# First four weight loads issued from ScalarE's queue instead of SyncE's, in a strided-attention and gated feed-forward kernel

## The chip, the cores and the metric

The kernel runs on one core of one Trainium2 chip. The metric is device time in microseconds (us) of one execution; the time of a kernel is the median over its runs. A smaller number is better.

## The reference, cut to what matters

Eight batches of eight heads attend over 576 positions with head size 64. Four heads use a local causal mask of 32 positions, four a strided causal mask. The heads are concatenated to a token matrix of 4608 x 512, which goes through two matrix products with a gate between them.

```python
scores = (1.0 / np.sqrt(D)) * np.matmul(q, k.transpose(0, 1, 3, 2))
mask_local = (rel >= 0) & (rel < 32)
mask_strided = (rel >= 0) & (pos[None, :] % 32 == pos[:, None] % 32)
attn = softmax(np.where(mask_of_head, scores, -1e9))
x = np.matmul(attn, v)            # rearranged to 4608 x 512
h = x @ w_in                      # 512 x 2048
g = h * np.clip(h + 3.0, 0.0, 6.0) / 6.0
out = g @ w_out                   # 2048 x 512
```

The two weight matrices come as 64-bit floats, q, k and v as 32-bit floats.

## The kernel before, in words

**Order of the work.** The kernel records every operation with the engines that may run it, a cost, a due time and the keys that it reads and writes (`op`, line 74). `Plan.emit` (line 91) then walks a list scheduler over the records, with the costs and due times as they are written, and so fixes the order of the instructions on each engine. The chip runs each engine's list strictly in that order; what an instruction really waits for is decided by semaphores. A change of one record's engine or cost can therefore move instructions on every engine, far from the record itself. Where the planner sees a gap on TensorE early on, it puts in a filler matmul on the identity (line 1580).

**Attention.** A pair is two heads of one batch. The pairs of batch 0 are worked in the order 0, 2, 1, 3 (`TURNS`); pairs 0 and 1 are local, 2 and 3 strided. For these four, q and k are loaded plainly and turned upright by TensorE (line 372), copied out of PSUM by ScalarE or VectorE (lines 514, 516), multiplied to scores (lines 605, 613), and the softmax goes back and forth: VectorE masks and takes the maximum (638, 652), GpSimd subtracts it (656), ScalarE takes the exponential (660), VectorE sums and inverts (666, 669), GpSimd normalises (673). For strided pairs ScalarE copies the scores out in four pieces for each head (631), and GpSimd adds the mask (648). The weights of the softmax are turned by TensorE and ScalarE for pairs 0 and 1 (372, 730) and by VectorE for pairs 2 and 3 (692). The product with v (389, 745) is written out as a high part by ScalarE (427) and a low part by VectorE (430); these are the tiles x.

**v of the first four pairs.** `load_v` (line 558) issues it from SyncE: six transfers for a local pair (lines 378 and 381), four for a strided one (line 567). These loads are recorded with the key "gate", which a small memset on VectorE (line 644) writes, so the planner puts none of them ahead of it.

**Weights.** `weight_part` (line 261) is called 32 times, for 16 blocks of w_in and 16 of w_out, in the order of `k`. One block is 128 x 512 in 64-bit floats. `load` (line 268) issues its transfer; the first sixteen blocks also wait for "gate" in the plan. The first four blocks (k below 4) are those of w_in for the first quarter of the hidden units; they have due times of their own. Then each block is turned into 32-bit floats by two ScalarE operations (282, 286) and one of VectorE (290, the join), and split into a high part (ScalarE 304 or GpSimd 306) and a low part (GpSimd 309).

**Feed-forward.** `ffn` (line 828) works batch 0 first: a chunk `fc` of 128 hidden units is the sum of four groups of three matmuls, one group for each pair's x (866, 867, 868, tile ph); the first four chunks are begun together. The gate is a ScalarE and a VectorE operation (786, 789); the result is split into a high part on ScalarE (800) and a low part on GpSimd (804, tile gl), and the second product goes to the tiles acc (843, 844, 845, of which 845 needs gl). Later batches are worked in the same manner or, for batches 3 to 7, by a recursive scheme with fewer products.

**Queues.** In the program before, SyncE issues all transfers but the k of the first two pairs, which ScalarE issues at the start. The transfers of both queues take turns on eight completion semaphores, so that each transfer waits for the one eight places earlier in the program.

## Time and profile before

| what | value |
|---|---|
| median of 3 runs | 872.61 us (871.39 to 873.68) |
| the profiled execution | 868.6 us, its span 866.8 us |
| mean granted TensorE clock in it | 0.997 |
| busy, of the span | TensorE 97%, GpSimd 71%, ScalarE 64%, VectorE 62% |
| bytes moved | 179.12 MB, mean 207 GB/s |

The profile shows one execution. PE is TensorE, DVE VectorE, ACT ScalarE, POOL GpSimd, and SPq and ACTq are the queues that issue transfers. In a row of the timeline stand the start, the duration, the engine, the line, the operation, the tile written and the tile read, the shape and the count; square brackets hold the idle time ahead of it and what ended that. Names such as L274 are lines of the kernel before; in the changed program all lines behind the new constant are one higher.

### The profile page before, as it was taken

What the parts mean: (1) busy time and instruction counts of PE and PEld (TensorE: products, weight loads), DVE (VectorE), ACT (ScalarE), POOL (GpSimd) and SP (SyncE); (2) the same over time, 40 slices, a digit from 0 to 9 for tenths busy, and PEclk for the clock granted to TensorE, in tenths of its full rate; (3) what the DMA queues carried; (4) which work ended last, traced back from release to release, by engine and by line L of the source; (5) the groups of instructions that cost most, each with busy time, mean ns of one, the idle gap of its engine ahead of it and who ended that gap; (6) DMA issues with size and microseconds to landing.
All of it is one profiled execution on the core that took longest, in us unless ns stands there. A gap on an engine that the chain in (4) does not pass through costs nothing.

```text
span 866.8 us, 18953 instructions
## 1 busy us (share of the span) xinstructions
PE 844.6 (97%) x6956; PEld 680.0 (78%) x6956; DVE 539.1 (62%) x899; ACT 558.8 (64%) x1240; POOL 615.8 (71%) x612
## 2 busy tenths in 40 slices
PE   9899999999999999999999999999999999999996
PEld 7667777878888887888888878788888778888884
DVE  6878877534444437554545663566767988555586
ACT  4777665877877965887768755777644645454441
POOL 5798785678448878676577995565974987767573
PEclk9999999999999999999999999999999999999998
DMA  6999714889874346889999998787666667866636
GB/s 156 314 210 271 195 32 119 250 246 286 251 201 115 104 118 170 230 222 249 264 251 266 341 287 226 212 240 195 183 200 184 193 179 222 242 197 194 182 122 146
DMA packets 323308, 179.12 MB, mean 207 GB/s; under 512 B 182864, under 2 KB 300368, under 8 KB 323216
## 3 DMA queue, kind: packets, MB, share of 16 engines
q1 hardware_dynamic: 318564, 176.27, 72.4%
q10 hardware_dynamic: 4652, 1.64, 0.9%
q8 instruction: 55, 0.90, 0.4%
q14 instruction: 37, 0.30, 0.1%
HBM read 136.97 MB, written 40.89 MB: 205 GB/s over the span
## 4 chain that ended last, share of the span: by engine, by line
PE 79%; POOL 7%; DVE 5%; ACT 3%; DMA 3%; issue 2%; SPq 0%; POOLq 0%; DVEq 0%; ACTq 0%
PE P L1139 9%; PE P L1141 8%; PE P L1140 8%; PE cP L1462 5%; PE cP L1463 5%; PE cP L1464 5%; PE acc L843 4%; PE acc L845 4%; PE acc L844 4%; PE ph L866 4%; PE ph L868 3%; PE ph L867 3%; PE acc L1224 3%; PE acc L1225 3%; PE acc L1226 3%; PE pv L400 2%
## 5 line engine op out<-in xcount | busy, mean ns | idle before, releaser
L1480 DVE SCALAR_TENSOR_TENSOR C<-cP,C 128x512 f32<-128x512 f32 x96 | 65.7, 687 | 40.3 <-PE cP L1464 39.5
L804 POOL TENSOR_TENSOR gl<-u,gh 128x512 fp32r<-128x512 f32 x48 | 64.6, 1351 | 23.9 <-ACT gh L800 13.2
L1151 DVE TENSOR_TENSOR G<-P,G 128x512 f32<-128x512 f32 x64 | 44.0, 689 | 57.9 <-PE P L1141 49.5
L845 PE MATMUL acc<-wo,gl 128*128 128x512 f32 x192 | 75.5, 393 | 2.5 <-POOL gl L804 2.2
L1139 PE MATMUL P<-B_T,wr 128*128 128x512 f32 x192 | 75.4, 393 | 2.3 <-DVE G L1151 1.6
L843 PE MATMUL acc<-wo,gh 128*128 128x512 f32 x192 | 76.9, 400 | 0.7 <-POOL wo L309 0.7
L844 PE MATMUL acc<-wo,gh 128*128 128x512 f32 x192 | 75.0, 391 | 0.2 <-POOL wo L309 0.2
L1141 PE MATMUL P<-B_T,wr 128*128 128x512 f32 x192 | 74.8, 389 | 0.0
L1140 PE MATMUL P<-B_T,wr 128*128 128x512 f32 x192 | 74.7, 389 | 0.0
L1377 POOL TENSOR_TENSOR sp<-G,sp 128x512 fp32r<-128x512 f32 x34 | 47.5, 1410 | 25.7 <-ACT sp L1373 25.7
L1146 ACT COPY G<-P 128x512 f32<-128x512 f32 x64 | 37.6, 587 | 43.4 <-PE P L1141 43.0
L673 POOL TENSOR_TENSOR e<-e,st 128x144 f32<-128x144 f32 (+1 forms) x64 | 43.6, 683 | 29.3 <-DVE st L669 21.2
L789 DVE SCALAR_TENSOR_TENSOR u<-u,ph 128x512 f32<-128x512 f32 x48 | 32.6, 681 | 42.0 <-ACT u L786 41.9
L866 PE MATMUL ph<-x,wi 128*128 128x512 f32 x128 | 52.3, 409 | 3.5 <-DVE u L789 1.9
L708 ACT COPY atloc<-e 32x192 f32<-32x192 f32 x144 | 50.8, 353 | 3.8 <-DVE e L698 1.4
L868 PE MATMUL ph<-x,wi 128*128 128x512 f32 x128 | 50.4, 394 | 1.1 <-POOL wi L309 1.1
L867 PE MATMUL ph<-x,wi 128*128 128x512 f32 x128 | 50.1, 391 | 0.4 <-DVE x L430 0.4
L666 DVE TENSOR_REDUCE st<-e 128x8 f32<-128x152 f32 (+1 forms) x64 | 26.9, 426 | 35.2 <-ACT e L660 18.9
L1139 PE MATMUL P<-B_B,wr 128*128 128x512 f32 x120 | 48.2, 401 | 0.1
L1140 PE MATMUL P<-B_B,wr 128*128 128x512 f32 x120 | 46.9, 390 | 0.0
L1141 PE MATMUL P<-B_B,wr 128*128 128x512 f32 x120 | 46.8, 390 | 0.0
L845 PEld LDWEIGHTS acc<-wo,gl 128*128 128x128 f32 x192 | 36.0, 188 | 12.2 <-POOL gl L804 4.6
(605 smaller groups left out, 2650.0 us busy)
## 6 DMA issues: line engine op xcount, KB each, us to landing
wr<-dA SPq DMA_DIRECT2D x72, 256.0 KB
or<-do SPq DMA_DIRECT2D x32, 512.0 KB
wr<-dSu SPq DMA_DIRECT2D x48, 256.0 KB
wr<-dSv SPq DMA_DIRECT2D x48, 256.0 KB
or<-do SPq DMA_DIRECT2D x48, 256.0 KB
rawi<-in_moe_w_in_dram SPq DMA_DIRECT2D x16, 512.0 KB
rawo<-in_moe_w_out_dram SPq DMA_DIRECT2D x16, 512.0 KB
do<-wo SPq DMA_DIRECT2D x16, 512.0 KB
```

The source lines that it names most:

```text
L708: nc.scalar.copy(at[PAD * (a + h):PAD * (a + h) + PAD, :, rows], e[rows, :, PAD * h:PAD * h + PAD])
L804: (nc.vector if tail else nc.gpsimd).tensor_tensor(out=to, in0=src(), in1=tiles[gk[0]].bitcast(F32), op=ALU.subtract)
L843: nc.tensor.matmul(acc, gh, woh, start=fc == 0, stop=False)
L844: nc.tensor.matmul(acc, gh, wol, start=False, stop=False)
L845: nc.tensor.matmul(acc, gl, woh, start=False, stop=end)
L866: nc.tensor.matmul(ph, wih, xh, start=n_ == 0, stop=False)
L867: nc.tensor.matmul(ph, wih, xl, start=False, stop=False)
L868: nc.tensor.matmul(ph, wil, xh, start=False, stop=n_ == NCC - 1)
L1139: nc.tensor.matmul(ph, wh, xh, start=fresh and k == 0, stop=False, skip_group_check=not fresh)
L1140: nc.tensor.matmul(ph, wh, xl, start=False, stop=False, skip_group_check=not fresh)
L1141: nc.tensor.matmul(ph, wl, xh, start=False, stop=k == 1, skip_group_check=not fresh)
L1480: nc.vector.scalar_tensor_tensor(out=tiles[ck], in0=tiles[bank], scalar=1.0 / 6.0, in1=tiles[ck], op0=ALU.mult, op1=ALU.add)
```

## The change

The loads of the first four weight blocks are recorded for ScalarE instead of SyncE, at a cost of 0.45 instead of 0.53 in the plan, and are issued from ScalarE's queue. Due times, reads, writes and all other records stay.

```diff
 AHEAD = 27.0
+ONACT = 4
 OPEN = 6.0
...
-            nc.sync.dma_start(raw, src.bitcast(I32).rearrange("p (n t) -> p n t", t=2))
+            (nc.scalar if k < ONACT else nc.sync).dma_start(raw, src.bitcast(I32).rearrange("p (n t) -> p n t", t=2))
...
-        op("SP", 0.53, load, reads=["gate"] if k < 16 else [], writes=[key], due=(-49, -48.99, -48.8, -48.79)[k] if k < 4 else ...)
+        op("ACT" if k < ONACT else "SP", 0.45 if k < ONACT else 0.53, load, reads=["gate"] if k < 16 else [], writes=[key], due=(-49, -48.99, -48.8, -48.79)[k] if k < 4 else ...)
```

What moves is seen in the programs. First ScalarE, at the start of pair 0's softmax, before; qt and kt are the upright q and k of pair 1, e0 and e1 the two heads' scores, ps0_20 and ps1_21 the raw scores of pair 2:

```order
L514 COPY qt0_1_255<-qp0_11_380 128x3x96
L514 COPY kt0_1_256<-kp0_10_403 128x3x96
L660 ACTIVATE e0_130<-e0_130 96x6x64
L631 COPY e0_130<-ps0_20_425 32x8x18 x4
L660 ACTIVATE e1_228<-e1_228 96x6x64
L631 COPY e1_228<-ps1_21_426 32x8x18 x4
```

And the same place of the changed program; rawi00 to rawi03 are the four weight blocks:

```order
L515 COPY qt0_1_255<-qp0_11_380 128x3x96
L275 DMA rawi00_423<-in_moe_w_in_dram 128x1024
L275 DMA rawi01_427<-in_moe_w_in_dram 128x1024
L275 DMA rawi02_464<-in_moe_w_in_dram 128x1024
L275 DMA rawi03_468<-in_moe_w_in_dram 128x1024
L661 ACTIVATE e0_130<-e0_130 96x6x64
L661 ACTIVATE e1_228<-e1_228 96x6x64
L632 COPY e0_130<-ps0_20_429 32x8x18 x4
```

The four issues stand ahead of pair 0's two exponentials, which now follow each other; the copy of kt that stood there went to VectorE.

On SyncE the v of the four pairs now stands in one row. This is the changed program from the second head of pair 0 on, with the semaphores that each transfer waits for; 0 to 7 behind DMAHW are the eight completion semaphores, and the weight blocks 00 to 03 hold numbers 0, 2, 4 and 6:

```order
L379 DMA v0_01_239<-in_v_dram 32x64 [waits DMAHW7_49]
L382 DMA v0_01_239<-in_v_dram 64x8x64 [waits DMAHW0_49]
L382 DMA v0_01_239<-in_v_dram 64x9x64 [waits DMAHW1_49]
L568 DMA v0_2_241<-in_v_dram 18x2x512 [waits DMAHW2_49]
L568 DMA v0_2_241<-in_v_dram 18x2x512 [waits DMAHW3_49]
L568 DMA v0_2_241<-in_v_dram 18x2x512 [waits DMAHW4_49]
L568 DMA v0_2_241<-in_v_dram 18x2x512 [waits DMAHW5_49]
L379 DMA v0_10_251<-in_v_dram 32x64 [waits DMAHW6_49]
```

Before, two weight loads stood between the v of pair 2 and that of pair 1, and two between pair 1 and pair 3. Now four of the v transfers wait until a weight block of the other queue has landed.

GpSimd, where the first low part of the gated result (gl0_0, for chunk 0) is made, before; wo is a block of w_out, wi10 and wi11 are blocks of the second quarter of w_in:

```order
L306 CAST wo02_985<-fo02_944 128x512
L309 TENSOR_TENSOR wo01_977<-fo01_915,wo01_977 128x512
L309 TENSOR_TENSOR wo02_985<-fo02_944,wo02_985 128x512
L309 TENSOR_TENSOR wo03_997<-fo03_983,wo03_997 128x512
L804 TENSOR_TENSOR gl0_0_1031<-u0_0_1009,gh0_0_1026 128x512
L804 TENSOR_TENSOR gl0_1_1036<-u0_1_1014,gh0_1_1029 128x512
L306 CAST wi10_1051<-fi10_999 128x512
L309 TENSOR_TENSOR wi10_1051<-fi10_999,wi10_1051 128x512
```

And in the changed program:

```order
L307 CAST wo03_996<-fo03_976 128x512
L310 TENSOR_TENSOR wo02_993<-fo02_951,wo02_993 128x512
L310 TENSOR_TENSOR wo03_996<-fo03_976,wo03_996 128x512
L307 CAST wi10_1009<-fi10_998 128x512
L310 TENSOR_TENSOR wi10_1009<-fi10_998,wi10_1009 128x512
L307 CAST wi11_1032<-fi11_1007 128x512
L310 TENSOR_TENSOR wi11_1032<-fi11_1007,wi11_1032 128x512
L805 TENSOR_TENSOR gl0_0_1054<-u0_0_1021,gh0_0_1045 128x512
L805 TENSOR_TENSOR gl0_1_1061<-u0_1_1029,gh0_1_1052 128x512
```

Two whole weight blocks now stand ahead of gl0_0. On TensorE one group each of chunks 4 and 5 now stands ahead of the first acc. On TensorE there are three filler matmuls more in all (15 instead of 12): three instead of one ahead of the transposes of pair 3's k, none instead of one between the two heads' turned softmax of pair 0, six instead of three ahead of pair 2's values, and two instead of three ahead of those of pair 1. On VectorE the copy of pair 3's k (line 516) now stands ahead of pair 2's first maximum (652) instead of behind it, and the first weight block's join (290) behind both of pair 1's sums (666) instead of ahead of the second. Small exchanges of neighbours go on through about the first 70% of each engine's list; behind that the order is the old one.

More of the change, by code (lines that the diff above doesn't have):

```diff
@@ L309, in lo @@
             nc.gpsimd.tensor_tensor(out=part(1), in0=whole(), in1=part(0).bitcast(F32), op=ALU.subtract)
-        op("SP", 0.53, load, reads=["gate"] if k < 16 else [], writes=[key], due=(-49, -48.99, -48.8, -48.79)[k] if k < 4 else -48.4 + 0.01 * k if k < 6 else -2 + 0.1 * k if k < 16 else due - 20.0, early=7.0 if k < 16 else due - 30.0, after=1.6 if k < 16 else 1.25)
+        op("ACT" if k < ONACT else "SP", 0.45 if k < ONACT else 0.53, load, reads=["gate"] if k < 16 else [], writes=[key], due=(-49, -48.99, -48.8, -48.79)[k] if k < 4 else -48.4 + 0.01 * k if k < 6 else -2 + 0.1 * k if k < 16 else due - 20.0, early=7.0 if k < 16 else due - 30.0, after=1.6 if k < 16 else 1.25)
         op("ACT", 0.68, high, reads=[key], writes=[fkey], due=due - 5, room=LATE + 1.0)
```

## The prediction

> **What bounds the kernel now.** I read the page first, for the bound of the whole, then the busy time by stage, then the timeline of the first 60 us, where the change lies. From the page, the share of TensorE and the chain that ended last:
>
> ```profile
> PE 844.6 (97%) x6956; PEld 680.0 (78%) x6956; DVE 539.1 (62%) x899; ACT 558.8 (64%) x1240; POOL 615.8 (71%) x612
> PE 79%; POOL 7%; DVE 5%; ACT 3%; DMA 3%; issue 2%; SPq 0%; POOLq 0%; DVEq 0%; ACTq 0%
> ```
>
> TensorE bounds the run. Only the parts of the chain outside it, all told a fifth, can be shortened, and most of them lie early. The busy time by stage, with columns from:to, length, the busy time of PE, PEld, DVE, ACT and POOL, the granted clock, the DMA share and GB/s:
>
> ```profile
> 15.00:23.00 8.00, 8.00 (x266) 6.46 (x259) 5.80 (x16) 4.77 (x16) 4.10 (x8) 1.00 0.66 165
> 23.00:30.00 7.00, 6.29 (x141) 4.54 (x136) 6.78 (x19) 4.71 (x11) 2.86 (x4) 1.00 0.93 229
> 30.00:50.00 20.00, 17.01 (x176) 11.81 (x175) 13.64 (x29) 15.35 (x37) 18.27 (x22) 1.00 1.03 367
> 51.00:54.00 3.00, 1.73 (x7) 0.88 (x6) 2.04 (x4) 3.00 (x6) 2.70 (x3) 1.00 0.62 94
> 60.00:100.00 40.00, 38.36 (x368) 29.50 (x369) 32.97 (x60) 25.80 (x48) 34.34 (x33) 1.00 0.86 223
> 140.00:840.00 700.00, 695.30 (x5149) 564.49 (x5148) 411.92 (x656) 464.60 (x1055) 496.50 (x476) 1.00 0.75 213
> ```
>
> The reader is to see three stages. From 23 to 30 us VectorE is the full engine (6.78 of 7). From 30 to 50 it is GpSimd (18.27 of 20), with the transfers at their limit (share 1.03, 367 GB/s). From 60 us on TensorE is idle for only 1.64 of 40 us, and for 4.7 of the 700 us from 140 to 840. TensorE's 8.00 of 8 at the start is not all work:
>
> ```profile
> L1580 PE MATMUL idle<-ident x24: 486/486/1009, 2.8 to 30.8; 128*128 128x384 f32 x24
> ```
>
> These are the fillers, up to 30.8 us. So the change can earn only what TensorE loses before about 60 us, and whatever it earns there must get past VectorE and then GpSimd.
>
> **SyncE's row.** The issues of v and of the first weights:
>
> ```profile
> 13.20 0.33 SPq L378 DMA_DIRECT2D v<-in_v_dram  x1
> 17.94 1.64 SPq L567 DMA_DIRECT2D v<-in_v_dram  x4
> 19.62 0.84 SPq L274 DMA_DIRECT2D rawi<-in_moe_w_in_dram  x2
> 20.50 1.67 SPq L378 DMA_DIRECT2D v<-in_v_dram  x1
> 25.66 2.34 SPq L274 DMA_DIRECT2D rawi<-in_moe_w_in_dram  x2
> 28.11 1.40 SPq L567 DMA_DIRECT2D v<-in_v_dram  x4
> 29.55 4.22 SPq L274 DMA_DIRECT2D rawo<-in_moe_w_out_dram  x4
> ...
> rawi<-in_moe_w_in_dram SPq DMA_DIRECT2D x16, 512.0 KB
> ```
>
> The two pairs of weight issues take 0.84 + 2.34 = 3.18 us. Without them the first w_out load goes from 29.55 to 26.4. Against this stand the new waits: four v transfers wait for a weight block to land, and the rest of SyncE's list, every later load, is queued behind them. Four blocks are 2.1 MB, 5.7 us at the 367 GB/s of the full stage. Issued from 13.6 on, the fourth lands at 19.3 at best, and v of pair 1, which waits for it, would come up at 19.6: nothing lost. At worst it shares with all that is moved from 15 to 23 now (165 GB/s, 1.3 MB): 3.4 MB, 9.3 us, 22.9, and 3.3 us are lost. So w_out starts between 26.4 and 29.7, and I take the middle, 28.0. GpSimd takes up the first w_out block only at 44.08 (below), 14.5 us after its issue, so that neither end is on the path. If that cover went, it would be worth 1.6 us.
>
> The Trainium skill, "DMA: Bandwidth & Descriptors", section "Issuing engines are not separate DMA queues", says that transfers started from several engines run on the same 16 DMA engines, and that a second issuing engine saves only the time of issuing. By that rule the whole change is worth at most those 3.18 us of SyncE. The row from 15 to 23 agrees only in part: with a DMA share of 0.66 there is also room into which weights can be moved.
>
> **ScalarE's row.** The place that takes the four issues, and the first use of a weight block:
>
> ```profile
> 12.36 1.19 ACT L514 COPY qt<-qp 128x288 f32<-128x288 f32 x2 [1.49 <-PE qp L372]
> 14.80 0.54 ACT L660 ACTIVATE e<-e 96x384 f32<-96x384 f32 x1
> 17.06 0.53 ACT L660 ACTIVATE e<-e 96x384 f32<-96x384 f32 x1
> ...
> 25.98 0.64 ACT L282 ACTIVATE fi<-rawi 128x512 f32<-128x512 f32 x1
> ```
>
> ScalarE is free at 13.55. At 0.42 us an issue (0.84 for two) it is done at 15.2, at 1.06 (4.22 for four, a full queue) at 17.8. I take 15.2, since the queue is empty. The first exponential starts at 15.2 instead of 14.80, the second at 15.8 instead of 17.06: pair 0 gains about a microsecond on GpSimd. At the other end the exponentials lose 3.0 and 1.3 us. The gain is not kept, since other engines' lists changed too.
>
> **Pair 2, on TensorE and VectorE.** One filler, three fillers, pair 2's first maximum, its second head's turning, and the first block's join:
>
> ```profile
> 16.94 0.91 PE L1580 MATMUL idle<-ident 128*128 128x384 f32 x2
> 23.71 2.20 PE L1580 MATMUL idle<-ident 128*128 128x384 f32 x6
> ...
> 18.09 0.29 DVE L652 TENSOR_REDUCE st<-e 128x8 f32<-128x144 f32 x1
> 25.09 1.75 DVE L692 STREAM_TRANSPOSE atstr<-e 32x256 f32<-32x256 f32 x4
> 28.57 1.26 DVE L290 SCALAR_TENSOR_TENSOR fi<-fi,rawi 128x512 int32<-128x512 int32 x1
> ```
>
> Three fillers (2.20) now run from 16.94, so pair 3's k is turned from 19.1. Its first half is there half a microsecond later, and VectorE's copy of it, about 0.5, ends near 20.2. Pair 2's first maximum, which now stands behind it, slips from 18.09 to 20.2, by 2.1. VectorE is full from then on, so the second head's turning ends at 28.9 instead of 26.84, and the join, now behind one more sum, starts at about 30.9 instead of 28.57, though the block has been in memory for some 10 us. At the least (the fillers hidden under the wait for VectorE's copies) the slip is 0.9.
>
> **GpSimd.** The low parts of the first block and of the block needed second, the block of w_out work, and the first two gl with what follows:
>
> ```profile
> 31.96 1.27 POOL L309 TENSOR_TENSOR wi<-fi,wi 128x512 fp32r<-128x512 f32 x1
> 39.41 1.29 POOL L309 TENSOR_TENSOR wi<-fi,wi 128x512 fp32r<-128x512 f32 x1
> 44.08 1.03 POOL L306 CAST wo<-fo 128x512 fp32r<-128x512 f32 x1 [0.80 <-issue]
> 46.79 0.64 POOL L306 CAST wo<-fo 128x512 fp32r<-128x512 f32 x1
> 47.39 4.30 POOL L309 TENSOR_TENSOR wo<-fo,wo 128x512 fp32r<-128x512 f32 x3
> 51.99 3.01 POOL L804 TENSOR_TENSOR gl<-u,gh 128x512 fp32r<-128x512 f32 x2 [0.30 <-ACT gh L800]
> 54.95 0.60 POOL L306 CAST wi<-fi 128x512 fp32r<-128x512 f32 x1
> 55.64 1.31 POOL L309 TENSOR_TENSOR wi<-fi,wi 128x512 fp32r<-128x512 f32 x1
> 61.52 0.82 POOL L656 TENSOR_TENSOR e<-e,st 128x144 f32<-128x144 f32 x2
> ```
>
> The first block starts late and the next ones are ready at once, so GpSimd closes its gaps: it has 1.7 idle us from 30 to 50 to close. I put the second-needed low part at 40.7 as before (39.41 + 1.29), between 39.0 and 42.2. Then come one more low part (1.29) and a normalising step (0.41): 42.4. The w_out work took from 44.08 to 51.69, 7.61 us; the new order has one more high part, 0.64, so it ends at 50.65. Two w_in blocks follow (0.60 + 1.31 each, 3.82) to 54.5, then the first gl (half of 3.01) to 56.0. TensorE at this place, and its pitch:
>
> ```profile
> 52.01 0.47 PE L843 MATMUL acc<-wo,gh 128*128 128x512 f32 x1 [0.65 <-POOL wo L309]
> 53.34 0.50 PE L845 MATMUL acc<-wo,gl 128*128 128x512 f32 x1 [0.62 <-POOL gl L804]
> 53.67 0.39 PE L843 MATMUL acc<-wo,gh 128*128 128x512 f32 x1
> 53.90 0.40 PE L844 MATMUL acc<-wo,gh 128*128 128x512 f32 x1
> ```
>
> The first matmul that needs gl moves from 53.34 to about 56.0, 2.6 later. By then TensorE has done two groups more (chunks 4 and 5), six matmuls of 0.23, 1.4 us. So it is 1.2 us behind. GpSimd, though, is ahead: it ends the second gl at 57.5 with 3.82 us of w_in done, which before would have ended at 55.0 + 3.8 = 58.8, so by 1.3. Of TensorE's 1.64 idle us from 60 to 100 I let this lead win back half, 0.8, between nothing and all.
>
> **The sum.** 1.2 - 0.8 = +0.4. The profiled execution took 868.6 us (span 866.8, 1.8 around it), 4.0 below the median of the runs shown. I forecast 869.0 for such an execution and 873.0 for the median. About 0.3%, 2.6 us, is what a measurement of this kernel can tell from no change: 870.0 to 875.2. The case's own range is +0.4 with -0.8 to +0.8 for the lead won back and -1.7 to +1.5 for GpSimd's place at 40.7, which hardly both end at their worst: 871.3 to 874.8.
>
> **The rivals.**
>
> Faster: the early weights reach TensorE. For it: the transfers have room (0.66), and the blocks' conversions, at 25.98 before, can start about 22.5. Against it: VectorE is full, and in its new order the join is late. If the slip is only 0.9 and GpSimd closes its 1.7, the first gl is ready at about 54.3: 1.0 late, against two groups of 1.4 done, and all of the 1.64 is won back: -2.0. If it is not late at all, -1.4 - 1.64 = -3.0, which is 869.6.
>
> Slower: GpSimd's detour ahead of the first gl. For it: the order puts 3.82 us there, and VectorE's joins now come in one row beside GpSimd, where such a step took 1.03 instead of 0.64 (44.08 and 46.79). If the seven w_out steps and four w_in steps each stretch by half of that 0.4, 2.2 is added to 1.2, and nothing is won back: +3.4, which is 876.0. It decides from the point where the first gl ends later than 53.3 + 1.4 + 2.6 = 57.3.
>
> No effect as meant: the v transfers wait for the weights' landing, and SyncE's list starts w_out at 29.7 as before. Since that is covered by 14 us, it gives the forecast's time.
>
> The later reshuffle: 4.7 idle us lie between 140 and 840. Exchanges of neighbours may open or close one such stall; that adds about 1 us either way and is in the range.
>
> **How the numbers follow.** I give 0.60 to the forecast with the no-effect case, 0.22 to the faster rival, 0.18 to the slower one. These are also the chances of under 870.0, between, and over 875.2. The predicted time is 873.0; the range goes from 869.4 (near the faster rival's end) to 876.0 (the slower one's price).
>
> **What would show it.** In the new profile: ScalarE's four issues near 13.6 to 15.2; the first w_out issue near 28; the first join on VectorE near 31; the first gl from 54.5 to 56; TensorE idle there for about 3 us; less than 1.64 idle from 60 to 100; transposes of pair 2 ending near 29. A first gl before 53, or one after 57.3, would make the forecast wrong, and so would stalls behind 140 us that add up to over 2.6 us more or less than 4.7.

## The result and the profile after

The changed kernel takes 874.99 us (median of 6 runs, 874.76 to 877.29), the kernel before 871.88 in the runs beside it (6, 868.3 to 873.68). The ratio is 1.0054, with an interval of 1.0038 to 1.007: slower by about 3.1 us. The profiled execution took 874.76 (span 872.9, mean granted clock 0.993). That of before took 868.6, 3.3 below its own median, so the two traces lie 6.2 apart, twice as far as the medians; a part of the prediction's reading hung on that, as will be seen.

The page of the changed kernel, the busy times and the engines' shares of the chain that ended last:

```profile
PE 850.1 (97%) x6962; PEld 684.3 (78%) x6962; DVE 541.1 (62%) x898; ACT 558.9 (64%) x1240; POOL 615.7 (71%) x613
PE 84%; DVE 5%; POOL 4%; DMA 3%; issue 2%; ACT 1%; SPq 0%; POOLq 0%; DVEq 0%; ACTq 0%
```

TensorE's busy time grew by 5.5 us for six recorded matmuls more; so some of it is the same work done slower. The stages show where (columns as in the prediction's table):

```profile
24.00:28.00 4.00, 1.87 (x71) 1.61 (x72) 3.20 (x9) 1.08 (x3) 0.69 (x2) 0.98 0.45 115
28.00:31.60 3.60, 3.60 (x7) 1.95 (x8) 3.20 (x8) 3.60 (x9) 1.18 (x2) 0.55 0.62 140
46.00:62.00 16.00, 12.67 (x73) 9.27 (x72) 12.36 (x17) 11.94 (x23) 14.45 (x14) 0.89 0.83 194
60.00:100.00 40.00, 37.80 (x397) 29.31 (x397) 34.74 (x60) 26.38 (x48) 31.97 (x30) 1.00 0.72 209
140.00:840.00 700.00, 695.42 (x5146) 564.15 (x5145) 410.11 (x651) 465.48 (x1056) 498.90 (x479) 1.00 0.75 213
```

Behind 140 us TensorE is idle for 4.58 of 700 us, as before (4.70). The loss is early: half of 24 to 28 is idle, behind it the granted clock falls to 0.55, and from 46 to 62 it is 0.89 with 3.3 us idle. The kernel before, in that last stretch:

```profile
46.00:62.00 16.00, 14.03 (x181) 10.37 (x180) 10.68 (x17) 13.99 (x27) 14.95 (x14) 1.00 0.95 191
```

It gets 181 matmuls done there, of all kinds, and has 2.0 us idle. I followed the loss along TensorE's list, by the start of the n-th matmul in both traces, fillers left out: the changed kernel is 3.9 us late from 45 to 47, and 6.7 late around 63. So there are two places, one before 45 (3.9) and one from 46 to 62 (2.8).

**The first place.** The issues, in the timeline of the changed kernel:

```profile
13.54 1.80 ACTq L275 DMA_DIRECT2D rawi<-in_moe_w_in_dram  x4
...
13.87 0.33 SPq L379 DMA_DIRECT2D v<-in_v_dram  x1
...
19.34 6.26 SPq L568 DMA_DIRECT2D v<-in_v_dram  x4
...
31.82 1.78 SPq L275 DMA_DIRECT2D rawo<-in_moe_w_out_dram  x4
```

ScalarE's four issues end at 15.34, as forecast. SyncE issues v of pair 0 from 13.87 on, in the same moment. Its last two transfers wait 1.1 us for the first weight block, and then SyncE stands for 6.26 us in the four issues of pair 2's v. Two of these four need the semaphore of a weight block (numbers 2 and 4); the longest wait there, 3.0 us, is put down to an earlier transfer of v. And TensorE, at pair 0's product with v:

```profile
23.45 0.30 PE L390 MATMUL pv<-at,v 64*64 64x32 f32 x2
25.45 0.30 PE L390 MATMUL pv<-at,v 64*64 64x32 f32 x4 [1.71 <-DMA v<-in_v_dram]
26.08 0.77 PE L390 MATMUL pv<-at,v 64*64 64x32 f32 x34 [0.33 <-DMA v<-in_v_dram]
27.20 0.67 PE L390 MATMUL pv<-at,v 64*64 64x32 f32 x32 [0.35 <-issue]
```

It waits 2.04 us for v of pair 0, for which the prediction's sum had no term. The DMA queues from 17 to 21 us say why. First the changed kernel, where q10 holds the weights and q1 the v transfers (packets, MB, share):

```profile
q10 hardware_dynamic: 398, 1.45, 93.7%
q1 hardware_dynamic: 235, 0.06, 6.5%
```

Then the kernel before in the same 4 us:

```profile
q1 hardware_dynamic: 1315, 0.57, 58.4%
```

The weights move 1.45 MB, and v 0.06 instead of 0.57. Of the 1315 packets before, 1183 are under 512 bytes, as those of pair 0's v are (about 0.3 MB); nearly all the others belong to pair 2's v, which the changed kernel issues later. The Trainium skill, "DMA: Bandwidth & Descriptors", section "Queues, rings and completion order", says that each DMA engine goes round the queues packet by packet. The rows agree in direction: 398 packets, of 3.6 KB on average, went against 235 of about 256 bytes, which is 1.7 to one and not far from turns; the queue with the small packets got a twenty-fifth of the bytes.

**The second place.** GpSimd's work ahead of the first gl, and TensorE's waits there, both in the changed kernel:

```profile
52.80 3.47 POOL L310 TENSOR_TENSOR wo<-fo,wo 128x512 fp32r<-128x512 f32 x2
56.21 0.61 POOL L307 CAST wi<-fi 128x512 fp32r<-128x512 f32 x1
...
58.82 1.30 POOL L310 TENSOR_TENSOR wi<-fi,wi 128x512 fp32r<-128x512 f32 x1
60.09 2.50 POOL L805 TENSOR_TENSOR gl<-u,gh 128x512 fp32r<-128x512 f32 x2
```

```profile
52.96 0.50 PE L867 MATMUL ph<-x,wi 128*128 128x512 f32 x1 [1.61 <-ACT x L428]
53.98 0.50 PE L868 MATMUL ph<-x,wi 128*128 128x512 f32 x1 [0.53 <-DVE x L431]
55.71 0.63 PE L868 MATMUL ph<-x,wi 128*128 128x512 f32 x1
61.40 0.50 PE L846 MATMUL acc<-wo,gl 128*128 128x512 f32 x1 [1.20 <-POOL gl L805]
```

The first gl is ready at 61.3, not at 56.0. TensorE meets three things on the way: pair 3's x (2.14), matmuls at 0.63 instead of 0.39 us while the clock is down, and then gl itself (1.20). Which of them costs the time can't be read from one trace: a wait for x that goes may only become a longer wait for gl.

### The profile page after: what moved, and what is told of

It reads as the page before. It is cut to its first block, busy times and chain, and to the rows that moved or that the text cites. A ratio compares the mean times of both kernels' runs of the same rounds, so it can differ in the third digit from the quotient of the medians.

```text
span 872.9 us, 18948 instructions
## 1 busy us (share of the span) xinstructions
PE 850.1 (97%) x6962; PEld 684.3 (78%) x6962; DVE 541.1 (62%) x898; ACT 558.9 (64%) x1240; POOL 615.7 (71%) x613
## 4 chain that ended last, share of the span: by engine, by line
PE 84%; DVE 5%; POOL 4%; DMA 3%; issue 2%; ACT 1%; SPq 0%; POOLq 0%; DVEq 0%; ACTq 0%
PE P L1140 8%; PE P L1141 8%; PE P L1142 8%; PE cP L1463 5%; PE cP L1465 5%; PE cP L1464 5%; PE acc L844 5%; PE ph L867 4%; PE acc L846 4%; PE acc L845 4%; PE ph L868 4%; PE ph L869 4%; PE acc L1225 3%; PE acc L1226 3%; PE acc L1227 3%; PE ps L614 2%
## 5 line engine op out<-in xcount | busy, mean ns | idle before, releaser
L805 POOL TENSOR_TENSOR gl<-u,gh 128x512 fp32r<-128x512 f32 x48 | 62.4, 1301 | 33.1 <-ACT gh L801 26.7
L674 POOL TENSOR_TENSOR e<-e,st 96x384 f32<-96x384 f32 (+1 forms) x64 | 42.8, 672 | 25.2 <-DVE st L670 25.2
L653 DVE TENSOR_REDUCE st<-e 96x6 f32<-96x384 f32 (+1 forms) x64 | 25.8, 416 | 39.7 <-POOL e L649 39.5
L787 ACT ACTIVATE u<-ph,three 128x512 f32<-128x512 f32 x48 | 32.9, 686 | 25.4 <-PE ph L869 23.2
```

The lines of the kernel that those rows point to most:

```text
L805: (nc.vector if tail else nc.gpsimd).tensor_tensor(out=to, in0=src(), in1=tiles[gk[0]].bitcast(F32), op=ALU.subtract)
```

## The experiments

Three theories, named so in the expectations. **Theory 1**: the loss is the first place; the early weight bytes crowd out v of pair 0. **Theory 2**: the loss is the changed order of the instructions, whoever issues the loads and whenever they move. **Theory 3**, formed after the first four runs: a block of TensorE's own instructions is fetched behind the weights, and TensorE stops until it has come. In most kernels below the planner's finished list is frozen and single entries are moved in it, so that all else stays in place (`w` are the four weight loads, `v` the loads of pairs 2, 1 and 3, `moved[n]` the entry taken out; in the diffs, `src` stands for its view as 32-bit pairs). The kernel before ran beside each group; its medians there are 871.77, 871.88, 872.19, 871.94 and 872.18.

### Order and loads taken apart

The order of the changed program, but all loads issued by SyncE at their places of before:

```diff
-            (nc.scalar if k < ONACT else nc.sync).dma_start(raw, src)
+            nc.sync.dma_start(raw, src)
...
+            if n == v[0]:
+                out += [moved[x] for x in (w[0], w[1], v[1], w[2], w[3], v[2])]
```

> Every engine keeps the instruction order of the changed kernel, but the four weight loads are issued by SyncE again, at the places that they had before (two behind the v of pair 2, two behind the v of pair 1). If the early weight transfers crowd out the v of pair 0 (theory 1), the values of pair 0 wait for no transfer and end near 23.5 instead of 27.9, the granted clock stays at 1.0 from 24 to 31, and of the 3.1 that the changed kernel loses at least 2 come back: 871 to 873. If the new order costs by itself (theory 2: more fillers ahead of the values of pair 2, another order on VectorE, GpSimd's join and subtraction behind two more copies), the time stays near 875 although v is on time.

878.29 (6 runs), ratio 1.0082 [1.0057, 1.0107]. The new order without the early weights is no better than with them, so a loss of this size comes without early bytes too. But the kernel has two waits of its own: in this order ScalarE's conversions come sooner than the late loads, and TensorE stops once for a reason that the last section takes up:

```profile
25.49 0.67 ACT L288 ACTIVATE fi<-rawi 128x512 f32<-128x512 f32 x1 [3.22 <-DMA rawi<-in_moe_w_in_dram]
...
26.26 0.67 PE L395 MATMUL pv<-at,v 64*64 64x32 f32 x32 [2.97 <-issue]
```

The order of before, with only the issuing engine of the four loads changed:

```diff
-            nc.sync.dma_start(raw, src)
+            (nc.scalar if k < 4 else nc.sync).dma_start(raw, src)
```

> The kernel before, with its order on every engine, and one thing changed: the four loads are issued by ScalarE, at the same places in the order of emission as SyncE's were (behind the v of pair 2 and of pair 1). It tells whether the other engine as issuer costs anything by itself. Theory 1: no, since the transfers start no earlier than v's; 870 to 872.5. Theory 2 says the same, 871 to 873. A time above 874 would mean that ScalarE's issues themselves, some 0.45 each in its own work, are the loss.

879.86 (6 runs), 1.0085 [1.0064, 1.0106]. Here no engine's compute order differs from before, and yet it loses as much as any kernel of this group. The timeline shows ScalarE's computing held by its own transfers:

```profile
24.64 0.35 ACTq L279 DMA_DIRECT2D rawi<-in_moe_w_in_dram  x1
...
25.10 0.32 ACT L665 ACTIVATE e<-e 128x144 f32<-128x144 f32 x1 [5.88 <-DMA v<-in_v_dram]
...
36.96 0.40 ACT L432 CAST x<-pv 128x288 fp32r<-128x288 f32 x1 [10.74 <-DMA rawo<-in_moe_w_out_dram]
```

An issue that must wait for a completion semaphore holds the arithmetic behind it, for 5.88 and 10.74 us. In the change the four issues take 1.80 us together and no arithmetic waits behind them.

ScalarE's issues behind its copies of pair 2's scores, in the changed order:

```diff
+            if n == at:
+                out += [moved[x] for x in w + v]
```

> The changed kernel, with ScalarE's four issues put behind its copies of pair 2's scores, 4 to 5 later (about 18.5 instead of 13.6), when all transfers of the v of pair 0 have been issued. Theory 1 (the weights' transfers crowd out v): the v of pair 0 lands as before the change, the values of pair 0 end by 24, and the time is 871 to 873. Theory 2 (the order costs): near 875. A third outcome, 873 to 875 with the v of pair 0 on time, would mean that the v of pair 2 is now the one that is crowded out.

877.13 (6 runs), 1.0065 [1.0042, 1.0087]. ScalarE again stands behind an issue, for 7.4 us, and TensorE 4.8 for ScalarE; so the kernel pays another price than the one it saves and doesn't tell the theories apart.

Only the first block early from ScalarE, the other three from SyncE at their old places:

```diff
-            (nc.scalar if k < ONACT else nc.sync).dma_start(raw, src)
+            (nc.scalar if k < 1 else nc.sync).dma_start(raw, src)
...
+            if n == v[0]:
+                out += [moved[x] for x in (w[1], v[1], w[2], w[3], v[2])]
```

> The changed kernel's order, with only the first weight block (512 KB) issued early by ScalarE and the other three by SyncE at their old places: one early block between none and four. Theory 1: the lateness of the v of pair 0 goes with the bytes in front of it, so about a quarter of the 4 by which the values of pair 0 are late, some 1, and the time 872 to 873.5. Theory 2: near 875, as with four blocks or with none.

877.86 (7 runs), 1.0068 [1.0043, 1.0094]. A quarter of the early bytes, and no part of the loss is gone; but ScalarE now waits 4.8 us for weights in all, and TensorE stops 1.78. Theory 1 is weakened by all four; but each of them has a new wait of its own, so none gives the order's price.

### v of pair 0 sooner, and the fillers

The gate and pair 0's v ahead of the weights, in the changed program:

```diff
+            if n == keep:
+                out += [moved[gate], moved[v0]]
```

> The changed kernel, with the v of pair 0 asked for about 2.7 sooner: the one-element write on VectorE that holds SyncE back stands ahead of the first addition on the scores instead of behind it. The weights stay where the change put them. Theory 1 (the loss is the late v of pair 0): its values wait for no transfer and end near 24.5 instead of 27.9, the clock stays at 1.0 from 27 to 31, and the time is 870 to 873. Theory 3, formed from the first four runs (a block of TensorE's instructions is fetched behind the weights' transfers): the values of pair 0 still stop after 40 of their 72 matmuls, now with no transfer of data to wait for, until 26 to 27, and the time is 873.5 to 876.

880.67 (6 runs), 1.0099 [1.0065, 1.0133]. Worse, but not through v: ScalarE's issues now had to wait for semaphores that v's transfers held, and its exponentials for them (7.68 us). The kernel spoilt its own question.

Fewer fillers, since TensorE seemed to stop at the same place of its list each time; in the changed program, in the third and fourth run of fillers one call instead of three and three instead of six:

```diff
+        want, run, out = {2: 1, 3: 3}, -1, []
```

> The changed kernel with the kernel before's number of fillers at two places: one call instead of three ahead of the k transposes of pair 3, three instead of six ahead of the values of pair 2. Theory 1: v of pair 0 lands as late as with the change, the values of pair 0 end at 27 to 28; the values of pair 2 start up to 2 sooner, since six matmuls of fillers fewer run at half clock; 873 to 874.5. Theory 2 (the new order, its fillers above all): most of the loss goes, 871 to 873.

877.62 (6 runs), 1.0066 [1.0042, 1.0091]: not better. The wait for v took the fillers' place (2.2 us).

The program before, with three calls instead of one in the run of fillers ahead of pair 3's k, as the change has it:

```diff
+        want, run, out = {2: 3}, -1, []
```

> The kernel before, with one change: three filler calls instead of one ahead of the k transposes of pair 3 on TensorE, as the changed kernel has them (1.3 more filler time at 17 to 19). The weights are loaded as before. Theory 3: TensorE passes the border of its instruction block some 1.3 later, so the next block is asked for when the two first weight blocks are already on the wires; the values of pair 0 stop inside for 2 to 3, the clock may halve behind it, and the time is 873 to 876. If no fetch is in play: the transposes are 1.3 later in a place with room, 871 to 872.5.

872.63 (12 runs), 1.0021 [0.9997, 1.0045]. The interval reaches from nothing to most of the loss, so this run settles little. The profiled execution, 876.0, has one stop of TensorE with nothing to wait for (2.37).

Both edits together, v first and fewer fillers:

```diff
+                out += [moved[gate], moved[v0]]
...
+        want, run, out = {2: 1, 3: 3}, -1, []
```

> Both edits together: the v of pair 0 asked for 2.7 sooner, and the fillers as in the kernel before at the two places. If late v, late instructions and fillers at half clock are all of the loss, nothing stops TensorE for more than 1 between 20 and 32, and the time is that of the kernel before or better, 868 to 872. If it stays above 874, the loss sits later, in the order of VectorE and GpSimd between 32 and 60.

880.36 (6 runs), 1.0101 [1.0077, 1.0125]. As v_first, for the same reason.

To have v early without holding ScalarE, SyncE issues all: the gate, pair 0's v and then the four weights, right behind its last early q or k:

```diff
-            (nc.scalar if k < ONACT else nc.sync).dma_start(raw, src)
+            nc.sync.dma_start(raw, src)
...
+            if n == last:
+                out += [moved[n] for n in [gate, v0] + w]
```

> The changed kernel's order on TensorE, VectorE, GpSimd and ScalarE, with all issues on SyncE: the one-element write that holds v back is placed near 4 instead of 13.8, so SyncE issues the v of pair 0 right behind q and k, and the four weight blocks right behind that (about 11 to 15), ahead of the other v. The weights are as early as with the change, but behind the v of pair 0 in one queue, and ScalarE issues none. Theories 1 and 3: v of pair 0 lands by 17, its values wait for no transfer; if the fetch of instructions still runs into the weights, an issue wait of up to 2 stays. 869 to 872.5. Theory 2: near 875.

876.53 (7 runs), 1.0054 [1.0035, 1.0073]. In the trace no wait for v is left, and the loss is the change's, so a late v is not needed for it. But other waits stand in its place, three stops of TensorE with nothing to wait for (1.6, 1.5 and 1.1 us), so that this run alone doesn't refute Theory 1.

The same with fewer fillers:

```diff
+        want, run, out = {2: 1, 3: 3}, -1, []
```

> The same with the kernel before's fillers at two places (one call instead of three ahead of the k transposes of pair 3, three instead of six ahead of the values of pair 2). If TensorE waits for nothing there, the fillers only stand in its way: 0 to 2 less than the run with all issues on SyncE. If they cover a wait, nothing changes, or the clock falls and it is up to 3 slower.

878.41 (6 runs), 1.0063 [1.0046, 1.0081]. No better.

The program before, with its gate and thus all of SyncE's early loads sooner:

```diff
+            if n == last:
+                out += [moved[gate], moved[v0]]
```

> The kernel before with its order on every engine, and only the one-element write that holds v back placed near 4 instead of 13.1: SyncE issues the v of pair 0, the v of pair 2, and behind them the first weights some 3 to 5 sooner, each in its old order. It tells whether sooner loads are worth anything to an order that isn't made for them. No wait of TensorE before 31 is for a transfer, so theories 1 and 2 say: within 1 of the kernel before, 870.5 to 873. Theory 3 allows a loss of 1 to 3 if the weights now meet a fetch of TensorE's instructions.

875.45 (12 runs, 867.66 to 880.85), 1.0033 [1.0007, 1.0059]. Earlier loads, same order, and it loses too, without a wait of TensorE for v, but with stops of TensorE that have no other cause in the profile (2.1 and 0.9 us). That was the first sign that early transfers cost something in the order of before as well.

### The bytes taken away

If the order has a price of its own, it must show when the four blocks hardly move any bytes. The changed program with an eighth of each of the four blocks loaded and zeros in the rest:

```diff
+            nc.gpsimd.memset(raw, 0)
-            nc.scalar.dma_start(raw, src)
+            nc.scalar.dma_start(raw[:, :TOK // 8], src[:, :TOK // 8])
```

> The changed kernel with its order on every engine and its four early issues from ScalarE, but each of the four transfers carries an eighth of its bytes (64 KB of 512 KB); the rest of the four weight blocks is zero, written by four memsets on GpSimd while that engine is idle, so 7/8 of these four blocks of w_in are left out of the computation. Nothing else changes. Theory 1 and theory 3 (bytes on the wires, in front of v or of TensorE's instructions): the values of pair 0 run without a wait and end near 24.5, the clock stays at 1.0 up to 50, and the time is 869 to 872. Theory 2 (the new order costs by itself): near 875.

875.4 (7 runs), 1.0039 [1.002, 1.0058]. Spoilt by its own edit: ScalarE's issues waited for the memsets on GpSimd, and its first exponential 4.98 us. The next three clear the tiles some 10 us earlier instead; first the changed program with an eighth:

```diff
+                raw = new(wp, key, [P, TOK, 2], I32, f"rawi0{k}")
+                nc.gpsimd.memset(raw, 0)
...
-            nc.scalar.dma_start(raw, src)
+                nc.scalar.dma_start(tiles[key][:, :TOK // 8], src[:, :TOK // 8])
```

> The changed kernel with its order on every engine and ScalarE's four early issues, each transfer with an eighth of its bytes (64 of 512 KB), as in the first run of this kind; the memsets that write the rest as zero now stand at 5 to 9 on GpSimd, where it is idle, so that they hold up no issue (in the first run they stood at 14.7 and held ScalarE until 18.6). 7/8 of four blocks of w_in are left out of the computation. Theories 1 and 3 (bytes on the wires): the values of pair 0 end near 24.5 with no wait, the clock stays at 1.0 until 40, 869 to 872. Theory 2 (the order costs by itself): still near 875, with TensorE's waits at 50 to 54 and 59 to 62 as in the changed kernel.

873.32 (12 runs), 1.0034 [1.0018, 1.0049]. With `TOK // 2`, half the bytes:

```diff
-                nc.scalar.dma_start(tiles[key][:, :TOK // 8], src[:, :TOK // 8])
+                nc.scalar.dma_start(tiles[key][:, :TOK // 2], src[:, :TOK // 2])
```

> The same with half of the bytes (256 of 512 KB in each of the four early transfers; the other half of the four blocks of w_in is zero, so left out). A step between: theories 1 and 3 place it between the changed kernel and the run with an eighth, v of pair 0 late by about half of 2; theory 2 sees no difference between the three.

873.92 (12 runs), 1.0035 [1.0017, 1.0053], between the eighth and the whole, and not to be told from either. And the program before with an eighth:

```diff
-                nc.scalar.dma_start(tiles[key][:, :TOK // 8], src[:, :TOK // 8])
+                nc.sync.dma_start(tiles[key][:, :TOK // 8], src[:, :TOK // 8])
```

> The kernel before with its order and its issues on SyncE, and an eighth of the bytes in the same four weight transfers (the rest zero by the same early memsets on GpSimd; 7/8 of the four blocks of w_in left out). It is the base for the two runs above: if the bytes matter to the kernel before too (theory 3: its next instruction block races with the two first weight blocks, and the profiled execution is one that won), its median falls to that of its best executions, 868 to 870, and its spread narrows. If they don't, 871 to 873. The difference to the changed kernel with an eighth is then the cost of the order alone: theory 2 says 3 or more, theories 1 and 3 say under 1.

869.92 (12 runs), 0.998 [0.9959, 1.0001]. Apart from the four memsets the lists of TensorE, VectorE, ScalarE and GpSimd in these two kernels are, by the names and shapes in their traces, those of the changed kernel and of the kernel before. Now the four kernels stand in a table of two by two, medians in us:

```
                 all bytes   an eighth   the bytes cost
order of before    871.94      869.92        2.0
order of after     874.99      873.32        1.7
the order costs      3.1         3.4
```

The order costs 3.4 us when v is not held up at all; the intervals of 1.0034 and 0.998 lie clear of each other. Combined as if they were independent, the two intervals leave that price open by an estimated 2.3 us either way. The order comes here with its issuer, ScalarE or SyncE. By their medians the bytes cost about the same in both orders, so that they cancel in the comparison. That they cost anything is less sure, since both differences are 0.0020 of the ratio and no larger than their intervals allow. In the trace with an eighth v of pair 0 is on time: the queue of v from 17 to 21 us reads

```profile
q1 hardware_dynamic: 1377, 0.59, 57.1%
```

as before the change, and there is no wait for v. So Theory 1 falls as the main cause: the crowding is real, but the loss stays without it. That it adds a microsecond to the change can't be excluded with these intervals. Theory 3 isn't the change's loss either, by these traces: the stop is 0.35 us in the changed kernel and 1.21 in the one with an eighth, and there the list is nearly on time again at 46 (below).

The program before with its first two weight loads behind v of pair 1, to see whether less crowding helps it:

```diff
+            if n == v1:
+                out += [moved[x] for x in w]
```

> The kernel before, with SyncE's first two weight loads put behind the v of pair 1 (six issues later, at about 23.5 instead of 19.6) and nothing else moved. Theory 3: TensorE's instruction block of 20.5 meets no weights, so the spread to the upper side goes, but ScalarE's first conversions (26.0 and 27.7) wait up to 1.5 for their bytes: 869 to 872.5. Without a race it can only lose: 872 to 874.

873.85 (12 runs, 867.37 to 879.23), 1.0032 [1.0007, 1.0057]. It doesn't help. In its trace ScalarE's first conversion waits 2.6 us for its bytes and TensorE 2.1 for a block of w_in, so this run doesn't tell what the kernel before pays for the bytes.

Where the order costs is now read from two kernels with the same few bytes, and profiled executions near their medians (872.99 and 869.66). By the start of the n-th matmul, as above, the changed order is 0.2 us late at 46.6, 2.98 from 64 to 70, and 3.4 at the end. So nearly all of it falls between 46 and 64, and what ScalarE's issues and the early stop did before is no part of it. GpSimd there, in the changed order:

```profile
43.78 0.66 POOL L315 CAST wo<-fo 128x512 fp32r<-128x512 f32 x1 [0.62 <-DVE fo L299]
...
46.45 1.05 POOL L315 CAST wo<-fo 128x512 fp32r<-128x512 f32 x1 [0.61 <-DVE fo L299]
...
49.76 3.46 POOL L318 TENSOR_TENSOR wo<-fo,wo 128x512 fp32r<-128x512 f32 x2
53.16 0.61 POOL L315 CAST wi<-fi 128x512 fp32r<-128x512 f32 x1
...
57.04 2.52 POOL L813 TENSOR_TENSOR gl<-u,gh 128x512 fp32r<-128x512 f32 x2
```

And in the order of before:

```profile
44.80 1.00 POOL L314 CAST wo<-fo 128x512 fp32r<-128x512 f32 x1 [0.78 <-issue]
...
48.09 4.30 POOL L317 TENSOR_TENSOR wo<-fo,wo 128x512 fp32r<-128x512 f32 x3
52.69 3.00 POOL L812 TENSOR_TENSOR gl<-u,gh 128x512 fp32r<-128x512 f32 x2 [0.30 <-ACT gh L808]
```

GpSimd begins the w_out work 1.02 us sooner in the changed order and ends it 0.83 later (53.22 against 52.39), with 9.44 us instead of 7.59. Then come the two w_in blocks, 53.16 to 57.04 = 3.88, and gl starts 4.35 later. TensorE's waits from 40 to 62 us, changed order:

```profile
PE ph L875 <- ACT x L436: 1.7, 1, 1.7
PE ph L877 <- POOL wi L318: 1.3, 1, 1.3
PE acc L854 <- POOL gl L813: 1.3, 1, 1.3
PE ph L876 <- DVE x L439: 0.5, 1, 0.5
```

The first matmul with gl starts at 58.37 instead of 54.03, 4.34 later; by then six more matmuls of 0.23 are done, 1.38. 4.34 - 1.38 = 2.96: this is the 2.98 by which the whole list is late. The two matmuls, the changed order first, and a stretch at half clock that its trace has ahead of them:

```profile
58.37 0.50 PE L854 MATMUL acc<-wo,gl 128*128 128x512 f32 x1 [1.29 <-POOL gl L813]
54.03 0.50 PE L853 MATMUL acc<-wo,gl 128*128 128x512 f32 x1 [0.62 <-POOL gl L812]
```

```profile
51.00:54.00 3.00, 3.00 (x7) 2.42 (x8) 1.62 (x2) 1.35 (x4) 2.92 (x4) 0.50 0.73 130
```

That TensorE still waits 1.3 for gl says that the waits ahead of it (1.7 and 0.5 for x) and the 3 us at clock 0.50 lay in GpSimd's shadow.

With all its bytes the changed kernel begins the w_out work at 46.84 instead of 43.78, 3.06 later again, and its matmuls are as much later at 62 to 100; behind 100 half of that is won back, and 1.5 is left at the end.

### Is it x, or GpSimd?

By the waits alone one would blame pair 3's x, the longest. So its halves are made sooner, with GpSimd's and TensorE's lists as in the changed program. VectorE's list, and then ScalarE's:

```diff
 SCALAR_TENSOR_TENSOR fo02<-fo02,rawo02 128x512
+TENSOR_TENSOR x0<-pv0,x0 128x4x4x16
 SCALAR_TENSOR_TENSOR fo03<-fo03,rawo03 128x512
...
 SCALAR_TENSOR_TENSOR fi10<-fi10,rawi10 128x512
-TENSOR_TENSOR x0<-pv0,x0 128x4x4x16
...
 CAST wo02<-fo02 128x512
+COPY left3<-pv0 128x4x4x2
+CAST x0<-pv0 128x4x4x16
 ACTIVATE fi10<-rawi10 128x512
-COPY left3<-pv0 128x4x4x2
 ACTIVATE rawi10<-rawi10 128x512
-CAST x0<-pv0 128x4x4x16
```

> The changed kernel with one place of its order mended: the two subtractions on VectorE that make the low part of pair 3's x stand ahead of the fourth w_out join and of the first join of the next quarter, and ScalarE's two copies of pair 3's second half ahead of the conversion of block 10. Loads, fillers and everything before 48 stay. If the order's cost sits in TensorE's wait for this x (1.6 and 0.5 in the profile of the changed kernel, at 51 to 54) and the halved clock behind it, some 1.3 of wait and 1.5 of clock come back: 871.5 to 873, about the kernel before. If the wait only moves to the gelu's gl on GpSimd at 60, or the order costs elsewhere: 874 to 876.

876.35 (10 runs), 1.0054 [1.0034, 1.0073], the change's own ratio. In its trace TensorE waits 0.2 for x and 2.1 for a block of w_in. And the same edit with an eighth of the four blocks:

```diff
+TENSOR_TENSOR x0<-pv0,x0 128x4x4x16
...
+CAST x0<-pv0 128x4x4x16
...
+                nc.scalar.dma_start(tiles[key][:, :TOK // 8], src[:, :TOK // 8])
```

> The same mend in the kernel with an eighth of the bytes in the four early transfers (7/8 of four blocks of w_in left out, as there). It closes the two by two: the order of the changed kernel cost 3.4 over the order of the kernel before at an eighth of the bytes (873.3 against 869.9). If the wait for pair 3's x and the clock behind it are that cost, 870 to 871; if not, near 873.

874.57 (12 runs), 1.0028 [1.0006, 1.0051], beside 1.0034 without the edit: nothing gained that could be told. The waits from 40 to 64 us of this kernel:

```profile
PE ph L875 <- POOL wi L315: 2.1, 1, 2.1
PE ph L877 <- POOL wi L318: 2.1, 2, 1.6
```

The 2.2 us for x are gone but for 0.17, and the same TensorE now waits 2.1 for block 10 of w_in, which GpSimd hasn't converted. The wait moved from one name to the next. GpSimd is the bound of this stage; x only stood in front of it.

No kernel here beats the kernel before with the full computation. One that would follow from the cause, the changed order with the first two gl put ahead of the blocks 10 and 11 on GpSimd, was not tried. By the rows above it would not be enough alone: TensorE's list has the groups of chunks 4 and 5 ahead of the first acc, and they need block 10, so these would have to move back as well. That the two blocks ahead of gl are the order's price is thus read from the rows and their sum; no run took them away.

## Why the prediction was wrong

I gave "within 0.3%" 0.60 and "slower" 0.18; it was slower by 0.54%, inside the range (869.4 to 876.0) but on the other side of the line. The time itself, 874.99, still lies 0.2 under the 875.2 that I drew as the line; that was drawn from a median of 872.61 in three runs, and beside the change the kernel before took 871.88 in six. What came is the rival **"Slower: GpSimd's detour ahead of the first gl"**: its condition (the first gl ends later than 57.3) is met with 61.3, and with 58.3 where few bytes move, and its price of 3.4 is the order's measured price. That the two agree to the digit is luck: the rival had stretched steps and no lead won back, and what came was made of other parts, as follows.

The step that failed is **the GpSimd term**, "the new order has one more high part, 0.64, so it ends at 50.65". The structure of the sum held: the delay of the first gl less the two groups done meanwhile. In the pair of kernels with few bytes, the delay was 4.34 instead of 2.6 and the groups 1.38 as forecast 1.4, so +2.96 instead of +1.2. Two parts make up the 1.7 by which the delay was larger, within 0.2:

- GpSimd was to win 1.7 us before the w_out work by closing its gaps (44.08 to 42.4). It won 1.02 (44.80 to 43.78), for it had to wait for VectorE's join, [0.62 <-DVE fo L299]. That is 0.7 of the difference. In the order of before the same step, too, begins about 0.1 us behind the end of VectorE's first join, so that the 0.80 us in the prediction's row, [0.80 <-issue], was no gap that GpSimd could close alone.
- The w_out work was to take 8.25. It took 9.44, and in the changed kernel 9.43 (46.84 to 56.27). A second wait for a join (0.61) and low parts that are longer together (6.42 against 5.96) make most of that 1.2. I had taken the duration of before, in which the joins behind the first are ready, into an order that packs the joins and GpSimd's steps next to one another. The rival saw the neighbourhood but put its price on stretched steps; half of it was waits.

The second term, **the lead won back** (-0.8), didn't come either: 2.98 late at 64 to 70 and 3.4 at the end, so +0.4. From 60 to 100 TensorE is idle for 2.20 us in the changed kernel, where I had asked for less than 1.64. Together, 1.8 more on the first term and 1.2 more on the second make +3.4 of the forecast's +0.4.

A third step was wrong, and cost the forecast little if anything: the lateness of pair 0's v was put at nothing. I bounded the landing of the weights by the bandwidth of both and never asked which queue would get it; the queue of v got 0.06 instead of 0.57 MB, and SyncE's longest wait for a transfer, 3.0 us, was for v and not for a weight block. But the bytes cost 1.7 in the changed order and 2.0 in the old one, as far as the medians can tell. The profiled execution of before, 868.6, hardly shows that price; its median does. That may also be why the two traces lie 6.2 apart where the medians lie 3.1. How before pays its 2.0 stays open: its 35 runs beside these kernels spread from 866.73 to 876.88, which would suit a race of transfers that comes out differently from run to run, but no trace here shows it.

Right were: ScalarE's issues (13.54 to 15.34); that SyncE's waits are covered, for the first w_out issue came at 31.82, later than forecast (28, 29.7 at worst), and no wait for a w_out transfer followed on any computing engine; nearly the first join (32.42 against 31) and pair 2's turning (30.94 against 29), 1.4 and 1.9 late; TensorE's idle time at the first gl (3.3 against 3); and the stalls behind 140 us (4.58 against 4.70). The granted clock, for which the sum had no term, fell twice; behind 28 it fell on fillers, and ahead of gl into GpSimd's shadow.

## What to carry to other kernels

When a change reorders the instructions of an engine that is almost full, price its row from the first new wait to the first result that the bound engine needs, with the waits for the producers that are now packed beside it, not with the durations of the old order. A gain of that engine counts only where its next partner is ready sooner as well. And before a wait is blamed, take it away: if the next name in the list shows the same microseconds, the bound lies behind both.

## What the runs showed of the hardware

**A transfer on a computing engine's queue can stop its arithmetic.** ScalarE stood 5.88 and 10.74 us in one kernel, and 7.4, 7.68, 6.5 and 4.98 in four others, each time behind an issue that waited. The change's saving of 3.18 us of SyncE's issuing time is small against that.

**Small packets lost to large ones.** 235 packets beside 398 of another queue were 4% of the bytes; in the kernel before, with no second queue of data beside it, v's queue moved 1315 packets in the same 4 us.

**TensorE stops at fixed places of its instruction list.** In the changed kernel and in six others of its order it stops behind the 40th of pair 0's 72 value matmuls, for 0.35 us in the change, 0.77 to 2.97 in the others, the most with the loads late. Over all kernels the stops of more than 0.3 us before 34 us stand behind the 444th, 698th, 950th, 1204th or 1458th of TensorE's recorded instructions (matmuls and weight loads), 252 or 254 apart, and a 16 KB packet of the instruction queue ends 1.3 to 1.7 us before TensorE goes on. In the kernel with the 2.97 us stop, the queue from 23.8 to 24.9 us:

```profile
q8 instruction: 1, 0.02, 5.4%
```

The Trainium skill, "Runtime: NRT & Kernel Launch", section "Instruction fetch mechanics", has 16 KiB or 256 instructions as the unit of the fetch, and calls the cost of the crossing mostly hidden. The packet agrees, and the spacing nearly. Hidden it wasn't everywhere: the stops took 2.97, 2.37, 1.78, 1.6 and 1.2 us in five kernels, all in the first 30 us. In the profiled executions of the kernel before and of seven others there was none. Why the fetch is hidden in one kernel and not in another stays open. One more stop, 2.59 us at 36.4 in the kernel with one early block, stands elsewhere and has no such packet ahead of it.

**The clock fell behind short waits.** In the changed kernel 2.4 us of idle time between 23.7 and 27.2 were followed by a mean granted clock of 0.55 from 28 to 31.6, and 2.1 us between 51 and 54 by 0.57 from 55 to 59. In the kernel with few bytes 2.2 us between 48 and 51 were followed by 0.50 from 51 to 54.
